# Feeding the feed-forward block product by product, and fewer doubled weight steps, in a fused attention and SwiGLU kernel

## The chip, the cores and the metric

The kernel runs on one core of one Trainium2 chip. The metric is the device time of one execution in microseconds (us). The engines are named as in the profile: PE is TensorE (matmul), PEld its weight loads, DVE is VectorE, ACT is ScalarE, POOL is GpSimd, SP the queue of SyncE.

## The reference

Attention with a threshold, followed by a feed-forward block of SwiGLU type, all results in float32:

```python
# q, k, v: (8 batches, 8 heads, 576, 64)
scores = scale * np.matmul(q, k.transpose(0, 1, 3, 2))
thresh = np.max(scores, axis=-1, keepdims=True) - tau
scores = np.where(scores >= thresh, scores, -1000000000.0)
scores = scores - np.max(scores, axis=-1, keepdims=True)
attn = np.exp(scores)
attn = attn / (np.sum(attn, axis=-1, keepdims=True) + 1e-09)
out = np.matmul(attn, v)
x = out.transpose(0, 2, 1, 3).reshape(4608, 512)
g = x @ w_gate                       # 512 x 1536
silu = g * (1.0 / (1.0 + np.exp(-g)))
val = x @ w_val                      # 512 x 1536
result = silu * val @ w_out          # 1536 x 512
```

The three weight matrices come as 64-bit floating-point numbers.

## The kernel before, in words

**Two programs in one.** The attention half runs in tiles of scores; the block (the feed-forward half) is cut into small pieces and put between them, so that PE has work while the other engines do the softmax of a tile. One block unit is 256 rows of x. There are 18 units. Each has six groups of two feature strips of 128: for each group a gate product sum (`pg`), then a value product sum (`pv`), each of eight products (two strips, four pieces of the 512 inputs). One such product is a matmul of 128x128 by 256 columns, and the profile counts two instructions for it. After the gate sums ACT writes tanh(g/2) and g/2 (L518, L519); after the value sums DVE computes (tanh + 1) x value (L525); and `gates` multiplies with g/2 on GpSimd (L537). The outputs of the first two units are 24 products of 512 columns each (`output`, L574); the others take a scheme of seven block products (`seven`, L607) for which sums of weights and of hidden values are formed first.

**The tiles.** This text counts tiles of scores from T0 in the order of the program. The loop at the end goes over segments (a pair of heads) and the tiles in them:

- T0 to T7: batch 0, the first two tiles of each of four pairs, in which weights arrive and no block work exists yet
- T8 to T19: batch 0 again, three tiles for each of the four pairs (T10, T13, T16 and T19 are the short ones, 64 query rows of each head, `t == NT`)
- T20 to T159: seven batches of four segments, each of four full tiles and then the short one (T24, T29, T34 and so on). In each segment there is one tile in which the attention-times-values products of the segment before (`xa`, L469, 72 instructions) also run.

In batch 0 the tiles are normalised and transposed on PE (`flip`: `tp` and `end`) and multiplied with v soon after (`attend_tile`). In the later batches DVE transposes them in blocks of 32 (L394).

**A tile** has these steps: scores on PE (L311 in batch 0, L303 later) into two PSUM tiles, of which there are only two; maximum on DVE (L338 or L326, then an exchange between partitions, L276); exponential on ACT (L345); multiplication by the mask on DVE with a sum (L349), which is the last reader of the scores; the reciprocal sum, and the scaling on ACT and POOL (L357, L355).

**How the block is fed.** `block` is a generator. It yields the cost of what it has put out, and `fill(n)` draws from it until a credit of n is used up. A product of 256 columns costs 1. The main loop calls `fill(part)` twice in each tile, with `part` from `pace`, which spreads the block work at hand over the tiles that are still to come. What is drawn beyond the credit is taken from the next tile's. Block matmuls use PSUM tiles of one pool of four (`ps_f`), shared with the transposes and the value products.

**How the weights come.** There are 24 pieces of 128x768 values. `fetch_weights` starts the transfer of a piece. `split_weights` takes its two 32-bit halves on ACT (L193, L194), into the destination and into one of two buffers (`los`). `join_weights` puts the bits together with three DVE operations (L200, L204, L207) and an addition on POOL (L209), which is the last reader of the buffer. Sixteen pieces are for gate and value weights, eight for output weights. In an ordinary tile one piece is split and one joined. In the short tiles of T8 to T19 two are joined and a second one is split at the end of the tile.

All four engine queues are written in the order in which the program calls the operations; no scheduler moves them.

Of the kernel before, what the change touches and what calls it, by code (L numbers as in the profile page):

```python
# [19 lines left out]
def kernel(  # L20
# [30 lines left out]
    nc = tc.nc  # L51
    P = 128
    B, H, S, D = q.shape
    NP = H // 2
    DM, DFF = w_gate.shape
    NCC = DM // P
    NF = DFF // P
# [7 lines left out]
    NT = SM // P  # L65
    SH = S // 2
    TC = 256
# [98 lines left out]
    NW = len(wpieces)  # L166
# [332 lines left out]
    def rows_of_products(j, cs, f, mat, name):  # L499
        n = cs.stop - cs.start  # L500
        ps = ps_f.tile([P, 512], F32, name=name, tag="psf")[:, 0:GR * n].rearrange("p (f n) -> p f n", n=n)
        x = xts[j].rearrange("p c t a r -> p c (t a r)")
        for i in range(GR):
            for c in range(NCC):
                nc.tensor.matmul(ps[:, i], wgv[:, mat, c, (f + i) * P:(f + i + 1) * P], x[:, c, cs],  # L505
                                 start=(c == 0), stop=(c == NCC - 1))
            if i < GR - 1:
                yield HCOST
        return ps

    def gate(j, cs, f, hts, gts):
        if f // 2 not in hts:
            hts[f // 2] = hp.tile([P, 2, TC], F32, name="ht") if j != ("full", 0) else hfirst[:, f:f + 2, :]
        gts[f] = gp.tile([P, GR, TC], F32, name="gt"), tp_.tile([P, GR, TC], F32, name="tn")
        need(NCC * ((f + GR - 1) * P // FW + 1))
        ps = yield from rows_of_products(j, cs, f, 0, "pg")

        nc.scalar.activation(gts[f][1], ps, AF.Tanh, scale=0.5)  # L518
        nc.scalar.activation(gts[f][0], ps, AF.Copy, scale=0.5)  # L519
        yield HCOST  # L520

    def value(j, cs, f, hts, gts):
        ps = yield from rows_of_products(j, cs, f, 1, "pv")
        gt, tn = gts.pop(f)
        nc.vector.scalar_tensor_tensor(out=hts[f // 2], in0=tn, scalar=1.0, in1=ps, op0=ALU.add, op1=ALU.mult)  # L525
        ungated.append((hts, f // 2, gt))
        if f == NF - GR and cs.stop == TC:
            del xts[j]
        if f >= NF - 2 * GR and not ready:

            gates()
        yield HCOST

    def gates():
        eng = nc.vector if attended else nc.gpsimd
        for hts, x, gt in ungated:
            eng.tensor_tensor(out=hts[x], in0=hts[x], in1=gt, op=ALU.mult)  # L537
        for hts, x, gt in ungated:
            if hts["seven"] and x >= NF2 // 2:

                ht = hts[x]
                x -= NF2 // 2
                fs = slice(2 * x, 2 * x + 2)
                h11, h21 = hts[x][:, :, 0:P], hts[x][:, :, P:2 * P]
                eng.tensor_tensor(out=hs3[:, fs], in0=h11, in1=h21, op=ALU.subtract)
                eng.tensor_tensor(out=h21, in0=h21, in1=ht[:, :, P:2 * P], op=ALU.add)
                eng.tensor_tensor(out=hs2[:, fs], in0=h21, in1=h11, op=ALU.subtract)
        ungated.clear()

    OF = 3  # L550

    def send(unit, i, ob):

# [11 lines left out]
    def output(unit):  # L565
        hts = hidden[unit]
        for i in range(TC // P):
            po = ps_f.tile([P, 512], F32, name="po", tag="psf")[:, 0:DM].rearrange("p (e n) -> p e n", e=2)
            for f in range(NF):
                if f % OF == 0:  # L570
                    if any(u[0] is hts for u in ungated):
                        gates()
                    need(NW)
                nc.tensor.matmul(po, hts[f // 2][:, f % 2, i * P:(i + 1) * P], wo[:, :, f, :],  # L574
                                 start=(f == 0), stop=(f == NF - 1))
                if f == NF - 1:
                    ob = op.tile([P, 2, DM], F32, name="ob")
                    nc.scalar.copy(ob[:, i].rearrange("p (e n) -> p e n", e=2), po)
                    send(unit, i, ob[:, i])
                if f % OF == OF - 1:  # L580
                    yield OCOST

    w11, w12, w21, w22 = (wo[:, e, f * NF2:(f + 1) * NF2, :] for f in range(2) for e in range(2))

# [8 lines left out]
    def seven(unit):  # L593

        hts = hidden[unit]
        if any(u[0] is hts for u in ungated):
            gates()
        ob = op.tile([P, 2, DM], F32, name="ob")
        o11, o12, o21, o22 = (ob[:, i, e * DM2:(e + 1) * DM2] for i in range(2) for e in range(2))

        def block_of(y, i):
            return lambda f: hts[(y * NF2 + f) // 2][:, f % 2, i * P:(i + 1) * P]

        def product(h, w):
            ps = ps_f.tile([P, 512], F32, name="po", tag="psf")[:, 0:DM2]
            for f in range(NF2):
                nc.tensor.matmul(ps, h(f), w[:, f, :], start=(f == 0), stop=(f == NF2 - 1))  # L607
            return ps

        def add(o, x, y):  # L610
            nc.vector.tensor_tensor(out=o, in0=x, in1=y, op=ALU.add)

        nc.scalar.copy(o12, product(block_of(0, 0), w11))
        yield SCOST
        nc.scalar.copy(o21, product(block_of(1, 1), ws4))
        yield SCOST
        add(o11, o12, product(block_of(1, 0), w21))
        for x in range(NF2 // 2):
            h12 = hts[NF2 // 2 + x][:, :, 0:P]
            nc.gpsimd.tensor_tensor(out=h12, in0=h12, in1=hs2[:, 2 * x:2 * x + 2], op=ALU.subtract)  # L620
        yield SCOST
        add(o12, o12, product(lambda f: hs2[:, f, :], ws2))
        yield SCOST
        add(o22, o12, product(lambda f: hs3[:, f, :], ws3))
        nc.gpsimd.tensor_tensor(out=o21, in0=o21, in1=o22, op=ALU.add)
        yield SCOST
        ps = product(block_of(0, 1), w12)
        add(o22, o22, ps)
        add(o12, o12, ps)
        send(unit, 1, ob[:, 1])  # L630
        yield SCOST
        add(o12, o12, product(block_of(1, 0), w22))
        send(unit, 0, ob[:, 0])
        yield SCOST

    EARLY = 4
    HCOST, OCOST, SCOST = NCC, OF * DM / TC, NF2 * DM2 / TC
    hidden = {}  # L640
    ready = deque()

# [3 lines left out]
    FIRST, SECOND = unit_of("full", 0), unit_of("full", 1)  # L646

    def cost(unit):
        outs = 0 if unit == FIRST else 4 * NF // OF * OCOST if unit == SECOND else 7 * SCOST
        return 2 * NF * HCOST + outs  # L650

    def outputs(unit):
# [153 lines left out]
    for n, seg in enumerate(segs):  # L806
        if NP <= n < 2 * NP:
            seg["v"] = segs[seg["i"]]["v"]
        for x, t in enumerate(seg["tiles"]):
            go = scores(seg, t)  # L810
            next(go)
            next(last, None)
            attends = prev is not None and x == 1
            products = iter(())
            attend_tile()
            next(go)
            next(last, None)
            flip()
            if n == NP and x == 0:
                attend_tile()  # L820
                give(n - 1)
            if n == 2 * NP and x == 1:
                give(n - 1)
            if attends and n > 2 * NP:
                if prev["i"] % NP == 0:
                    need(NW)
                    start_batch(prev["i"] // NP)
                products = attend(prev)
            part = pace(n, x) / 2
            more = len(split)  # L830
            if n or x:
                split_weights()
                fetch_weights(2)
            if x == 0 and n >= NP:
                fetch_qk(seg["i"] + 1)
            next(go)
            if more and not (t == NT and NP <= n < 2 * NP):
                join_weights()
            fill(part)
            next(go)  # L840
            fill(part)
            gates()
            last = go
            if n == NP and later:
                to, fr = later.pop(0)
                nc.vector.transpose(out=to, in_=fr)
            if t == NT and NP <= n < 2 * NP:

                join_weights(2)
                split_weights()  # L850
                fetch_weights(2)
            if attends and n > 2 * NP:
                next(products)
                next(products)
                give(n - 1)
            if attends and seg["halved"]:
                load_v(seg)
            if x == 0 and 0 < n < NP:
                load_v(seg)
            if x == len(seg["tiles"]) - 2 and n + 1 < len(segs):  # L860
                prepare(segs[n + 1])
                if n < NP:
                    fetch_qk(segs[n + 1]["i"] + 1)
        prev = seg
# [42 lines left out]
```

## Time and profile before

| | before |
|---|---|
| time, median of 3 runs | 1526.37 us (1525.08 to 1527.90) |
| span of the profiled execution | 1524.4 us |
| PE busy | 1483.4 us (97%) |
| PEld busy | 1126.8 us (74%) |
| DVE busy | 995.6 us (65%) |
| ACT busy | 726.8 us (48%) |
| POOL busy | 645.5 us (42%) |
| gate and value products on PE (L505) | 399.8 + 399.9 us |
| seven-product outputs on PE (L607) | 176.2 us |
| scores on PE (L303) | 157.5 us |
| attention times values on PE (L469) | 128.8 us |

PE is nearly full over the whole span, so a shorter time can only come from where it is not, or from where its clock is low. The page's second part cuts the span into 40 slices of about 38 us, with the busy tenths of each engine and the clock that PE was granted. A table of windows gives the same for stretches that one chooses; a line of waits gives the engine and line that waited, what it waited for, the sum in us, how often, and the longest; the chain of waits goes back from the last instruction, or from the end of a window, to what released each step.

### The profile page before, as it was taken

The numbers are of one execution on the slowest core, as the hardware profiler recorded it, in microseconds if no ns is written. First come the engines' busy times: TensorE is split into PE (matmuls) and PEld (weight loads), VectorE is DVE, ScalarE is ACT, GpSimd is POOL, SyncE is SP. The second block draws the span as 40 slices with busy tenths as digits, with TensorE's granted clock in tenths as the row PEclk, the third lists the DMA queues.
The fourth block names the chain that finished last, engine by engine and source line by source line (L and its number), as shares of the span: only waits on it lengthen the run. The fifth ranks groups of instructions, "written<-read, shape, count | busy, mean of one in ns | idle before, by whom it ended". The sixth has DMA issues, their size and how long they took to land.

```text
span 1524.4 us, 31468 instructions
## 1 busy us (share of the span) xinstructions
PE 1483.4 (97%) x11784; PEld 1126.8 (74%) x11784; DVE 995.6 (65%) x3038; ACT 726.8 (48%) x2157; POOL 645.5 (42%) x638
## 2 busy tenths in 40 slices
PE   7998899899999999999999999999999999999999
PEld 5776564477777777787777777777777777888887
DVE  6877888867767777756666676767676776512212
ACT  5877555545445455444545545544544454311100
POOL 3355543348453545435444545444545353500000
PEclk9999999999999999999999999999999999999999
DMA  9543221111212011111101121211101120000000
GB/s 195 143 146 104 63 46 46 46 40 32 46 18 53 11 31 46 46 32 32 28 22 45 33 46 32 46 32 46 31 21 28 46 48 15 1 15 1 14 14 15
DMA packets 176872, 66.93 MB, mean 44 GB/s; under 512 B 159696, under 2 KB 159696, under 8 KB 176720
## 3 DMA queue, kind: packets, MB, share of 16 engines
q1 hardware_dynamic: 169552, 56.45, 16.3%
q0 software_dynamic: 2432, 7.87, 1.4%
q8 instruction: 94, 1.54, 0.4%
q10 hardware_dynamic: 4736, 0.59, 0.3%
q14 instruction: 58, 0.48, 0.1%
HBM read 55.44 MB, written 9.44 MB: 43 GB/s over the span
## 4 chain that ended last, share of the span: by engine, by line
PE 89%; DVE 6%; ACT 2%; issue 1%; DMA 1%; POOL 1%; SPq 0%; DVEq 0%; ACTq 0%; POOLq 0%
PE pv L505 23%; PE pg L505 23%; PE po L607 19%; PE sc L303 9%; PE xa L469 8%; PE po L574 2%; PE sc L311 1%; DVE pall L349 1%; PE tp L417 1%; DVE mx L326 1%; DVE pall L394 1%; PE xa L443 1%; ACT pall L345 1%; DVE mx L276 1%; DVE wo L207 0%
## 5 line engine op out<-in xcount | busy, mean ns | idle before, releaser
L355 POOL TENSOR_SCALAR pall<-pall,ri 128x288 f32<-128x288 f32 (+1 forms) x260 | 265.9, 1032 | 319.7 <-DVE ri L365 289.7
L505 PE MATMUL pg<-xall,wgv 128*128 128x256 f32 x1728 | 399.8, 382 | 0.7 <-ACT pall L423 0.6
L505 PE MATMUL pv<-xall,wgv 128*128 128x256 f32 x1728 | 399.9, 382 | 0.0
L505 PEld LDWEIGHTS pg<-xall,wgv 128*128 128x128 f32 x1728 | 323.5, 190 | 67.0 <-issue 20.6
L505 PEld LDWEIGHTS pv<-xall,wgv 128*128 128x128 f32 x1728 | 324.5, 190 | 63.3 <-issue 20.5
L326 DVE TENSOR_REDUCE mx<-sc 128x2 f32<-128x576 f32 x252 | 180.2, 750 | 205.7 <-PE sc L303 204.1
L349 DVE SCALAR_TENSOR_TENSOR pall<-sc,th,pall 128x288 f32<-128x288 f32 (+1 forms) x540 | 258.1, 528 | 33.2 <-ACT pall L345 33.2
L345 ACT ACTIVATE pall<-sc,nm 128x288 f32<-128x288 f32 (+1 forms) x540 | 236.8, 511 | 0.6
L341 ACT ACTIVATE th<-nm,cut 128x4 f32<-128x4 f32 (+1 forms) x140 | 41.6, 297 | 373.2 <-DVE nm L330 373.2
L537 POOL TENSOR_TENSOR ht<-ht,gt 128x512 f32<-128x512 f32 x84 | 106.8, 1271 | 212.1 <-DVE ht L525 137.4
L394 DVE STREAM_TRANSPOSE pall<-pall 128x576 f32<-128x576 f32 x252 | 181.4, 754 | 0.1
L607 PE MATMUL po<-wo,ht 128*128 128x256 f32 x768 | 176.2, 382 | 0.0
L303 PE MATMUL sc<-kT,qT 64*32 64x288 f32 x4032 | 157.5, 410 | 17.4 <-DVE pall L349 16.1
L525 DVE SCALAR_TENSOR_TENSOR ht<-tn,pv 128x512 f32<-128x512 f32 x102 | 69.9, 685 | 155.1 <-PE pv L505 148.6
L607 PEld LDWEIGHTS po<-wo,ht 128*128 128x128 f32 x768 | 144.3, 190 | 27.7 <-issue 5.6
L518 ACT ACTIVATE tn<-pg 128x512 f32<-128x512 f32 x108 | 64.8, 600 | 152.0 <-PE pg L505 145.5
L357 ACT ACTIVATE pall<-pall,ri 128x288 f32<-128x288 f32 (+1 forms) x264 | 132.8, 553 | 0.0
L279 ACT COPY sums<-sums 32x4 f32<-32x4 f32 (+1 forms) x560 | 108.5, 194 | 48.5 <-DVE pall L349 37.8
L469 PE MATMUL xa<-pall,vall 64*64 64x288 f32 x2016 | 128.8, 405 | 0.2 <-ACT pall L345 0.2
L303 PEld LDWEIGHTS sc<-kT,qT 64*32 64x32 f32 x4032 | 59.0, 105 | 94.2 <-issue 68.8
L469 PEld LDWEIGHTS xa<-pall,vall 64*64 64x64 f32 x2016 | 75.9, 133 | 49.0 <-issue 4.1
L620 POOL TENSOR_TENSOR ht<-ht,xall 128x256 f32<-128x256 f32 x48 | 34.6, 729 | 168.9 <-PE po L607 166.9
(101 smaller groups left out, 1338.5 us busy)
## 6 DMA issues: line engine op xcount, KB each, us to landing
vall<-in_v_dram SPq DMA_DIRECT2D x112, 144.0 KB, 3.4
qraw<-in_q_dram SPq DMA_DIRECT2D x116, 72.0 KB, 2.4
kraw<-in_k_dram SPq DMA_DIRECT2D x116, 72.0 KB, 2.8
out_dram<-ob POOLq DMA_DIRECT2D x28, 256.0 KB, 2.4
wo<-in_moe_w_gate_dram SPq DMA_DIRECT2D x16, 384.0 KB, 3.6
wo<-in_moe_w_val_dram SPq DMA_DIRECT2D x16, 384.0 KB, 4.3
xall<-in_moe_w_out_dram SPq DMA_DIRECT2D x5, 768.0 KB, 4.8
wo<-in_moe_w_out_dram SPq DMA_DIRECT2D x3, 768.0 KB, 4.6
```

Source lines behind the costliest of these rows:

```text
L279: nc.scalar.copy(out, in_[:, :, 0])
L303: nc.tensor.matmul(ps[g * G:(g + 1) * G, h, 0:SH], qT[hs, col + a * G:col + (a + 1) * G], kT[hs, c * SH:(c + 1) * SH], start=True, stop=True)
L326: nc.vector.tensor_reduce(out=mx[:, 2 * x:2 * x + 2, 0], in_=tile_[:, :, 0:SH], axis=AX.X, op=ALU.max, negate=True)
L345: nc.scalar.activation(ps[x], scs[x], AF.Exp, bias=nm[:, x:x + 1])
L349: nc.vector.scalar_tensor_tensor(out=ps[x], in0=scs[x], scalar=th[:, x:x + 1], in1=ps[x], op0=ALU.is_ge, op1=ALU.mult, accum_out=sm[:, x, ...
L355: nc.gpsimd.tensor_scalar(out=ps[x], in0=ps[x], scalar1=ri[:, x:x + 1], scalar2=None, op0=ALU.mult)
L357: nc.scalar.activation(ps[x], ps[x], AF.Copy, scale=ri[:, x:x + 1])
L394: nc.vector.transpose(out=p, in_=p)
L469: nc.tensor.matmul(xa[a][h * D:(h + 1) * D, at:at + n * G].rearrange("d (i q) -> d i q", q=G), vr[rs, h, j, :], p[rs, lo:lo + n, j, :], st ...
L505: nc.tensor.matmul(ps[:, i], wgv[:, mat, c, (f + i) * P:(f + i + 1) * P], x[:, c, cs], start=(c == 0), stop=(c == NCC - 1))
L537: eng.tensor_tensor(out=hts[x], in0=hts[x], in1=gt, op=ALU.mult)
L607: nc.tensor.matmul(ps, h(f), w[:, f, :], start=(f == 0), stop=(f == NF2 - 1))
```

## The change

The generator now yields after every product in place of after four products (gate and value sums), three output products of 512 columns (`output`, cost 6) or six products of the seven-product scheme (cost 6). The sums of the costs are the same. It is for spreading the block evenly over the tiles, which before got multiples of four or six.

The doubled weight step is kept only in the short tiles of the first two segments of batch 0 (T10 and T13); T16 and T19 become ordinary tiles, with one split and one join. Where the step is doubled, it now stands ahead of `gates()`, so that the additions of the join come before the gate multiplications in POOL's queue.

```diff
@@ rows_of_products
             for c in range(NCC):
                 nc.tensor.matmul(ps[:, i], wgv[:, mat, c, (f + i) * P:(f + i + 1) * P], x[:, c, cs],
                                  start=(c == 0), stop=(c == NCC - 1))
-            if i < GR - 1:
-                yield HCOST
+                if (i, c) != (GR - 1, NCC - 1):
+                    yield 1
         return ps
@@ gate, value
-        yield HCOST
+        yield 1
@@ output
             for f in range(NF):
-                if f % OF == 0:
-                    if any(u[0] is hts for u in ungated):
-                        gates()
-                    need(NW)
+                if any(u[0] is hts for u in ungated):
+                    gates()
+                need(NW)
...
-                if f % OF == OF - 1:
-                    yield OCOST
+                yield OCOST
@@ seven
             for f in range(NF2):
                 nc.tensor.matmul(ps, h(f), w[:, f, :], start=(f == 0), stop=(f == NF2 - 1))
+                if f < NF2 - 1:
+                    yield SCOST
             return ps
...
-        nc.scalar.copy(o12, product(block_of(0, 0), w11))
+        ps = yield from product(block_of(0, 0), w11)
+        nc.scalar.copy(o12, ps)
         yield SCOST
...
-    HCOST, OCOST, SCOST = NCC, OF * DM / TC, NF2 * DM2 / TC
+    HCOST, OCOST, SCOST = NCC, DM / TC, DM2 / TC
@@ main loop
             next(go)
-            if more and not (t == NT and NP <= n < 2 * NP):
+            double = t == NT and NP <= n < NP + 2
+            if more and not double:
                 join_weights()
             fill(part)
             next(go)
             fill(part)
+            if double:
+
+                join_weights(2)
+                split_weights()
+                fetch_weights(2)
             gates()
             last = go
             if n == NP and later:
                 to, fr = later.pop(0)
                 nc.vector.transpose(out=to, in_=fr)
-            if t == NT and NP <= n < 2 * NP:
-
-                join_weights(2)
-                split_weights()
-                fetch_weights(2)
```

More of the change, by code (lines that the diff above doesn't have):

```diff
@@ L531, in value @@
             gates()
-        yield HCOST
+        yield 1
     def gates():
@@ L548, in gates @@
         ungated.clear()
-    OF = 3
     def send(unit, i, ob):
@@ L611, in add @@
             nc.vector.tensor_tensor(out=o, in0=x, in1=y, op=ALU.add)
-        nc.scalar.copy(o12, product(block_of(0, 0), w11))
+        ps = yield from product(block_of(0, 0), w11)
+        nc.scalar.copy(o12, ps)
         yield SCOST
-        nc.scalar.copy(o21, product(block_of(1, 1), ws4))
+        ps = yield from product(block_of(1, 1), ws4)
+        nc.scalar.copy(o21, ps)
         yield SCOST
-        add(o11, o12, product(block_of(1, 0), w21))
+        ps = yield from product(block_of(1, 0), w21)
+        add(o11, o12, ps)
         for x in range(NF2 // 2):
@@ L621, in seven @@
         yield SCOST
-        add(o12, o12, product(lambda f: hs2[:, f, :], ws2))
+        ps = yield from product(lambda f: hs2[:, f, :], ws2)
+        add(o12, o12, ps)
         yield SCOST
-        add(o22, o12, product(lambda f: hs3[:, f, :], ws3))
+        ps = yield from product(lambda f: hs3[:, f, :], ws3)
+        add(o22, o12, ps)
         nc.gpsimd.tensor_tensor(out=o21, in0=o21, in1=o22, op=ALU.add)
         yield SCOST
-        ps = product(block_of(0, 1), w12)
+        ps = yield from product(block_of(0, 1), w12)
         add(o22, o22, ps)
@@ L631, in seven @@
         yield SCOST
-        add(o12, o12, product(block_of(1, 0), w22))
+        ps = yield from product(block_of(1, 0), w22)
+        add(o12, o12, ps)
         send(unit, 0, ob[:, 0])
@@ L648, in cost @@
     def cost(unit):
-        outs = 0 if unit == FIRST else 4 * NF // OF * OCOST if unit == SECOND else 7 * SCOST
+        outs = 0 if unit == FIRST else 4 * NF * OCOST if unit == SECOND else 7 * NF2 * SCOST
         return 2 * NF * HCOST + outs
```

## The prediction

> **What bounds the kernel now.** I read the slices of the page first, to see where TensorE (PE) is not full:
>
> ```profile
> PE   7998899899999999999999999999999999999999
> DVE  6877888867767777756666676767676776512212
> PEclk9999999999999999999999999999999999999999
> ```
>
> From the ninth slice on (38 us each) PE is at 90% or more; VectorE (DVE) is fuller before it than after. The table of windows puts numbers to that, with stage borders that I chose: the first eight tiles, the rest of batch 0 (T8 to T19), the first six tiles of batch 1 (T20 to T25), the rest of batch 1, batches 2 to 7, the tail.
>
> ```profile
> 0.00:62.00 62.00, 50.23 (x367) 37.41 (x368) 46.26 (x104) 43.63 (x95) 20.66 (x18) 1.00 0.81 185
> 62.00:153.00 91.00, 82.89 (x598) 64.01 (x596) 69.32 (x135) 68.69 (x133) 48.24 (x27) 0.96 0.37 120
> 153.00:196.00 43.00, 35.83 (x337) 25.03 (x342) 38.63 (x116) 25.62 (x72) 25.13 (x19) 0.96 0.34 74
> 196.00:310.00 114.00, 105.81 (x954) 57.46 (x958) 88.39 (x299) 62.97 (x207) 41.60 (x40) 0.99 0.18 42
> 310.00:1330.00 1020.00, 1017.78 (x8615) 777.03 (x8608) 708.61 (x2302) 502.99 (x1602) 499.29 (x520) 1.00 0.15 34
> 1330.00:1525.00 195.00, 190.80 (x934) 165.89 (x933) 44.43 (x85) 22.95 (x50) 10.61 (x15) 1.00 0.04 12
> ```
>
> Columns after the length: busy us of PE, PEld, DVE, ACT, POOL, then PE clock. PE idles 8.1, 7.2 and 8.2 us in the second to fourth row and 2.2 us in the 1020 us after; the first row has no block products and the last idles at the very end, so the change reaches neither. PE waits from 62 to 310 us:
>
> ```profile
> PE sc L303 <- DVE pall L349: 14.1, 9, 3.4
> PE sc L311 <- DVE pall L349: 7.2, 3, 4.6
> PE sc L303 <- PE sc L303: 0.8, 5, 0.2
> PE pg L505 <- ACT pall L423: 0.6, 1, 0.6
> ```
>
> Nearly all is one thing: the scores of the next tile wait until the multiplication by the mask (L349) has read the scores of this one. That PSUM pair is fully used by one tile, so PE gets past it only if its block products last as long as the chain of maximum, exponential and mask. The chain of waits for the longest of them:
>
> ```profile
> 125.63 0.69 DVE extra L525
> 126.32 2.02 DVE wo L200 x2
> ...
> 131.05 1.63 POOL wo L209
> 132.68 0.02 issue
> 132.70 0.99 ACT extra L194
> ...
> 134.03 0.64 ACT pall L345
> 134.67 0.02 issue
> 134.70 0.84 DVE pall L349 x2
> 135.53 0.14 issue
> 135.67 3.28 PE sc L311 x9
> ```
>
> A doubled join (DVE 126.3 to 131.0) comes before GpSimd's addition; the second split on ScalarE (ACT, L194) waits for that addition to free its buffer, and the exponential of the next tile stands behind it. Meanwhile PE had only four products and waited 4.62 us.
>
> **What the Trainium skill says.** "PSUM — Partial Sum Buffer", section Engine vs sequencer instructions: ACT, DVE and GpSimd queues are strict FIFO, and matmuls start and complete in program order. The chain above agrees: exponentials for a tile that was ready stand 1.6 us behind L194. "TensorE: Matmul & The Clock Gate", part 1, What's actually happening: after an idle window of about 3.4 us the PE clock goes to half, and comes back after a busy one. The trace agrees: clock 0.50 over 135.6 to 142.4 us (after the 4.62 us wait), 0.51 over 162.8 to 166.2 (after 3.37) and 0.50 over 299.4 to 302.8: 13.6 us at half, 6.8 us lost. "Perfetto Trace Analysis", Optimization Strategy: repeating bubbles on an engine that should be saturated can mean that PSUM for the next tile ran out. Here that is the score pair.
>
> **The change part by part.**
>
> *Single products, counted.* In the trace a product of 128x128 by 256 columns takes 3.45/8 = 0.43 us (tail, start to start); an output product of 512 columns counts as two. Per tile, before: T9 to T20 get 8 8 4, 8 8 4, 8 8 4, 8 8 4; T21 to T26 get 8 12 8 12 8 8. After, by the changed program's issue order: 7 7 7, 7 6 7, 7 7 7, 7 6 7 and 10 9 10 9 10 9; in T27 to T41 the spread of 6 to 12 becomes 8 to 10, and later 8 to 18 becomes 13 to 15 almost everywhere. Sums agree within 4 products at stage borders. No product is added; the few switches between scores and block keep their number, so I cost the finer steps themselves at nothing.
>
> *T8 to T19.* To win: 8.1 us idle and 3.4 of clock, 11.5. The waits ahead of T12, T15, T18 (1.55, 1.00, 4.62) follow the tiles of four products. The doubled joins of T16 and T19 go; a single join (0.5+0.5+0.9 plus gaps, 2.1 us of DVE) then sits ahead of L525, no second split stands in ACT's queue, and a tile there is 3.5 us of scores, transposes and values plus 7 x 0.43 = 6.5 us of PE, against 4.6 us from the start of the scores to the end of both L349 (68.57 to 73.2). So T18's wait and its slow clock vanish. T12 and T15 keep doubled joins: three products more in the tile ahead take 1.3 us, but two fewer come in the tiles before that, so I leave 0.65 and 0.55. In T10 the multiplication L525 now lies ahead of the join on DVE (+0.6), which is in that 0.65. The join ahead of GpSimd's gate multiplications (1.28 us each) keeps these off L209, for which ACT waits; they are read only by outputs about 100 us later: nothing.
>
> *A new wait here:* a half-done sum holds one of four PSUM buffers through the flip, which wants four. PE then stands in order behind ACT's copy, as at T12 (0.62). I count 0.6 and 0.3 as they stand in T12 and T15, and as new 0.6, 0.5 and 0.3 in T10, T16 and T18; bounds zero and twice the new ones. What remains is 0.65 + 0.55 + 0.9 + 1.4 = 3.5 us. T20 starts with two products fewer done (0.9). Gain 11.5 - 3.5 - 0.9 = 7.1.
>
> *T20 to T25.* Here DVE is busy 38.6 of 43 us, so it sets the pace. A full tile costs it 5.73 us from scores to scores (212.15 to 217.88: maxima 1.3, sums and exchange 1.2, transposes 1.35, two of four masks 0.9, start 0.8). A join adds 2.1, L525 0.6. The two joins taken from T16 and T19 now come in T22 and T24. Following DVE tile by tile: T20 6.5 (PE sets it, the 3.37 us wait gone), T21 7.55, T22 8.4, T23 7.9, T24 and T25 together 13.6, in sum 43.9 against 43.0 (152.99 to 195.94). Three more products are done (1.3). Gain 0.4: what T20 wins is paid back. PE may wait 3.3 us in T22 and lose its clock, but it has slack there.
>
> *T26 to T41.* A tile of ten products is 1.13 + 4.3 = 5.4 us for PE, so DVE's 5.73 sets it; where both k and q are transposed and a short tile follows, the pair takes about 12.0 (with L525) or 11.0 us. Tiles with the 72 value products (4.53) are PE's own. Credited with the products done: T26 +0.2, T27 to T30 24.7 to 23.4 with two fewer, +0.4; T31 +0.5; T32 to T36 33.5 to 31.7 with two fewer, +0.9; T37 to T41 37.0 to 32.4, +4.6, of which 1.7 is the clock loss at 299.4. Gain 6.7, rounded up from these.
>
> *Later.* 2.2 us of idle in 1020; with 13 products at least in every tile I expect about 1.6 of it. The yields inside the seven products of an output only move their place between tiles; PE stays full.
>
> Sum: 7.1 + 0.4 + 6.7 + 1.6 = 15.8 us, less a little for waits that I can't see: 1526.4 - 15.4 = 1511.0.
>
> **The rivals.** *A, DVE keeps the time.* Even products bring nothing where the DVE chain sets the pace, half-done sums stand in the way, and only the two removed doubled joins count: 4.62 idle + 3.4 clock, minus 0.9: 1519. For it: DVE 88.4 of 114 us busy in T26 to T41. Against it: DVE waits there for scores (3.35 us at 206.46, 0.8 at most others), after overfull tiles. *B, all idle is won:* 8.1 + 7.2 + 8.2 + 2.2 and 6.8 of clock, 32.5: 1494. Against it: 38.6 of 43 us DVE, with two joins more. *C, slower:* PSUM buffers held by half sums cost the copy wait of 0.6 in each of the 12 flips and of the 28 tiles with value products (24 us), which eats the 15.4: 1535. For it: one such wait exists. Against it: half sums were held in every second tile before, and the wait shows once. *D, no change,* 1526: gain and buffer waits cancel.
>
> **How the numbers follow.** Main 0.66, A 0.19, B 0.05, C 0.06, D 0.04. Faster: main, A and B, 0.90. The low end: if the 3.5 us left in T8 to T19 vanish, and T26 to T41 give all of their 8.2 idle and 1.7 of clock in place of 6.7, it is 6.7 us less, 1504.3, rounded to 1505. The high end takes in A, 1520. Outside lie B, C, D and the edges of the main case, about 2 in 10.
>
> **What would show it.** In the changed profile: PE busy unchanged near 1483 less the slow-clock time (about 5 us); no half clock at 135; no wait of PE over 1 us between T16 and T20; PE waiting 2 to 3 us ahead of T23 and T24 on L349, with a join just before; waits under 2 us ahead of T27 to T41, each after a short tile or a tile of eight products. A row of PE pg or pv waiting for ACT L423 or DVE L525 of more than 4 us in total would make C's mechanism real; idle in the batches 2 to 7 above 4 us would make the forecast wrong, and so would scores of T26 that start later than 192 us (195.94 before).

## The result and the profile after

| | before | changed |
|---|---|---|
| time, median of 6 runs each | 1527.13 us (1525.08 to 1528.51) | 1514.70 us (1513.19 to 1516.52) |
| span of the profiled execution | 1524.4 us | 1512.9 us |

The ratio is 0.992, with a 95% interval of 0.9907 to 0.9933: faster by 12.4 us, under one per cent but clear of the noise. The forecast was 1511.0 us with a range of 1505 to 1520.

The page of the changed kernel, the row of busy times and three rows of the 40 slices:

```profile
PE 1480.5 (98%) x11784; PEld 1121.3 (74%) x11784; DVE 994.8 (66%) x3038; ACT 727.1 (48%) x2157; POOL 643.3 (43%) x638
...
PE   7999899999999999999999999999999999999999
...
DVE  6878988777777777747767666776666767512212
...
PEclk9999999999999999999999999999999999999999
```

After the first slice only the fifth (151 to 189 us) has PE under 90%; it is also the one in which DVE stands at 90% or more. The table of windows with the same kind of borders (columns as before: length, busy us of PE, PEld, DVE, ACT, POOL, clock, DMA share, GB/s):

```profile
62.00:152.00 90.00, 85.11 (x663) 63.85 (x662) 70.42 (x141) 68.97 (x136) 48.65 (x28) 1.00 0.37 120
152.00:192.00 40.00, 33.48 (x296) 23.04 (x300) 36.99 (x113) 27.21 (x74) 22.54 (x18) 0.96 0.40 87
192.00:310.00 118.00, 113.22 (x1035) 60.54 (x1020) 94.03 (x316) 68.64 (x227) 44.88 (x43) 1.00 0.18 40
310.00:1318.00 1008.00, 1007.50 (x8509) 770.33 (x8510) 703.06 (x2282) 497.03 (x1581) 496.92 (x518) 1.00 0.16 34
```

PE now idles 4.9, 6.5, 4.8 and 0.5 us in these rows; before it was 8.1, 7.2, 8.2 and 2.2. The clock is down in one of these rows instead of three; one more stretch at half clock lies ahead of them (last section). The waits of PE from 62 to 310 us:

```profile
PE sc L303 <- DVE pall L349: 10.1, 12, 2.6
PE pv L505 <- ACT pall L423: 2.7, 3, 1.4
PE sc L303 <- PE sc L303: 0.9, 6, 0.2
PE sc L311 <- DVE pall L349: 0.9, 1, 0.9
```

Three things are to be seen. The waits of batch 0 for the mask (L311) fall from 7.2 us to 0.9. A new row of 2.7 us has come: value sums wait for ACT to empty a PSUM buffer. And the waits of the later batches (L303) are more in number, 12 for 9, but shorter.

The same in lengths from the start of one tile's scores to another's, in the profiled executions. This table also holds the experiments, and the next section refers to it:

| kernel | time, us | ratio to before (95%) | T8 to T20 | T20 to T26 | T26 to T42 | T42 to end |
|---|---|---|---|---|---|---|
| before | 1527.13 | 1 | 95.82 | 42.95 | 114.64 | 1213.84 |
| changed | 1514.70 | 0.992 (0.9907 to 0.9933) | 89.02 | 43.38 | 110.50 | 1211.56 |
| e1_single_only | 1517.30 | 0.9933 (0.9921 to 0.9945) | 92.03 | 43.90 | 110.50 | 1211.55 |
| e2_joins_only | 1521.66 | 0.996 (0.9948 to 0.9973) | 90.06 | 43.12 | 112.99 | 1213.80 |
| e3_coarse_batch0 | 1514.61 | 0.9917 (0.9903 to 0.993) | 88.86 | 42.52 | 110.95 | 1211.55 |
| e4_coarse_late | 1515.05 | 0.9918 (0.9906 to 0.993) | 89.25 | 43.42 | 110.50 | 1212.25 |
| e5_gates_first | 1515.32 | 0.9921 (0.9908 to 0.9935) | 90.25 | 43.39 | 110.50 | 1211.54 |
| e6_no_double | 1513.75 | 0.991 (0.9897 to 0.9923) | 84.32 | 45.53 | 112.23 | 1211.53 |
| e7_joins_t26 | 1516.40 | 0.9927 (0.9914 to 0.9939) | 89.56 | 40.15 | 116.81 | 1211.52 |
| e8_coarse0_joins_t26 | 1516.72 | 0.9925 (0.9913 to 0.9938) | 90.01 | 39.29 | 115.68 | 1211.54 |
| e9_hold_two_t26 | 1514.89 | 0.9917 (0.9901 to 0.9933) | 89.17 | 40.38 | 114.29 | 1211.52 |
| e10_nodouble_hold_one | 1511.73 | 0.9895 (0.9878 to 0.9913) | 84.32 | 45.57 | 110.30 | 1211.51 |
| e11_nodouble_hold_two | 1515.12 | 0.9916 (0.99 to 0.9932) | 84.33 | 45.29 | 112.92 | 1211.54 |
| e12_no_turn | 1516.24 | 0.9926 (0.9903 to 0.9949) | 89.17 | 43.39 | 110.56 | 1211.55 |

Each ratio is taken against runs of the kernel before beside it on the same chip (medians of these: 1527.66 for e1 to e4, 1527.82 for e5 to e8, 1526.57 for e9 to e12). Between before and changed the stages differ by -6.80, +0.43, -4.14 and -2.28 us; T8 itself starts 1.28 us later, 0.93 of it for a reason in the last section. The sum, -11.5, is the difference of the spans.

### The profile page after: what moved, and what is told of

Read it like the earlier page. It is cut to its first block, busy times and chain, and to the rows that moved or that the text cites. A ratio compares the mean times of both kernels' runs of the same rounds, so it can differ in the third digit from the quotient of the medians.

```text
span 1512.9 us, 31439 instructions
## 1 busy us (share of the span) xinstructions
PE 1480.5 (98%) x11784; PEld 1121.3 (74%) x11784; DVE 994.8 (66%) x3038; ACT 727.1 (48%) x2157; POOL 643.3 (43%) x638
## 5 line engine op out<-in xcount | busy, mean ns | idle before, releaser
L355 POOL TENSOR_SCALAR pall<-pall,ri 128x288 f32<-128x288 f32 (+1 forms) x260 | 265.9, 1032 | 344.8 <-DVE ri L365 317.9
L505 PE MATMUL pv<-xall,wgv 128*128 128x256 f32 x1728 | 404.9, 383 | 3.0 <-ACT pall L423 2.7
L326 DVE TENSOR_REDUCE mx<-sc 128x2 f32<-128x576 f32 x252 | 180.6, 751 | 237.4 <-PE sc L303 236.6
L349 DVE SCALAR_TENSOR_TENSOR pall<-sc,th,pall 128x288 f32<-128x288 f32 (+1 forms) x540 | 258.1, 528 | 31.6 <-ACT pall L345 31.6
L537 POOL TENSOR_TENSOR ht<-ht,gt 128x512 f32<-128x512 f32 x84 | 107.1, 1275 | 193.1 <-DVE ht L525 109.6
L394 DVE STREAM_TRANSPOSE pall<-pall 128x576 f32<-128x576 f32 x252 | 181.4, 754 | 2.8 <-POOL pall L355 2.8
L303 PE MATMUL sc<-kT,qT 64*32 64x288 f32 x4032 | 158.4, 411 | 11.3 <-DVE pall L349 10.1
L525 DVE SCALAR_TENSOR_TENSOR ht<-tn,pv 128x512 f32<-128x512 f32 x102 | 69.9, 685 | 132.3 <-PE pv L505 119.0
L303 PEld LDWEIGHTS sc<-kT,qT 64*32 64x32 f32 x4032 | 58.8, 106 | 89.0 <-issue 61.0
```

The lines of the kernel that those rows point to most:

```text
L303: nc.tensor.matmul(ps[g * G:(g + 1) * G, h, 0:SH], qT[hs, col + a * G:col + (a + 1) * G], kT[hs, c * SH:(c + 1) * SH], start=True, stop=True)
L326: nc.vector.tensor_reduce(out=mx[:, 2 * x:2 * x + 2, 0], in_=tile_[:, :, 0:SH], axis=AX.X, op=ALU.max, negate=True)
L349: nc.vector.scalar_tensor_tensor(out=ps[x], in0=scs[x], scalar=th[:, x:x + 1], in1=ps[x], op0=ALU.is_ge, op1=ALU.mult, accum_out=sm[:, x, ...
L355: nc.gpsimd.tensor_scalar(out=ps[x], in0=ps[x], scalar1=ri[:, x:x + 1], scalar2=None, op0=ALU.mult)
L394: nc.vector.transpose(out=p, in_=p)
```

## The experiments

**Which half does what: e1 and e2.** The first keeps the single products and puts the joins back, the second the reverse.

```diff
e1, against the changed kernel
-            double = t == NT and NP <= n < NP + 2
-            if more and not double:
+            if more and not (t == NT and NP <= n < 2 * NP):
...
-            if double:
-
-                join_weights(2)
-                split_weights()
-                fetch_weights(2)
             gates()
...
+            if t == NT and NP <= n < 2 * NP:
+
+                join_weights(2)
+                split_weights()
+                fetch_weights(2)
e2, against the changed kernel (value, output and seven likewise)
-                if (i, c) != (GR - 1, NCC - 1):
-                    yield 1
+            if i < GR - 1:
+                yield HCOST
```

> Single products as in the changed kernel; doubled joins in T10, T13, T16 and T19, behind the gate multiplications, as before. My theory: from T26 on it is the changed kernel (6 us of gain there), but T18 keeps a wait of about 3.5 us (4.6 less three products) with the slow clock behind it, and T21 one of about 2; T22 to T25 have two joins fewer than the changed kernel. 1517 to 1520 us. Rival 'the joins are the change': 1523 or more. Rival 'the single products are all': within 1 us of the changed kernel (1514.7).

> Steps of four and six products as before; doubled joins only in T10 and T13 and ahead of the gate multiplications, as in the changed kernel. My theory: the 4.62 us ahead of T18 and its slow clock go (8 us), T21's wait halves, T23 to T25 pay for the two later joins (3 to 4 us), T26 to T41 and later stay as before: 1519 to 1522 us. Rival 'the joins are the change': 1515. Rival 'the single products are all': 1526.

The stages part cleanly. With single products alone, T26 to T42 and all after are the changed kernel's to 0.01 us, and T8 to T20 wins 3.8 us. With the joins alone, T42 to the end is that of before, and T8 to T20 wins 5.8. A stretch at half clock (114.6 to 118.0 us) is in that one: T15 takes 9.08 us where e3, with the same steps there, takes 7.83. Without these 1.25 us it would be 88.8, the changed kernel's 89.0. e3 below, which is e2's program up to T19, has no such stretch and takes 88.86. So in batch 0 the joins do all of it, and the single products are one of two cures for the same wait: the 4.62 us ahead of T18's scores are gone in e1, in e2 and with both. Inside T18 PE waits 1.53 us in e1, 0.62 in e2 and 0.57 with both. That is why 10.4 us (e1) and 6.0 (e2) are together 12.4 and not 16.4. (e1's time came inside its range, but the wait of 3.5 us ahead of T18 that was expected with it did not come.) PE's waits in e1 from 62 to 200 us show what single products bring with them while the joins stay doubled:

```profile
PE pv L505 <- ACT pall L423: 2.9, 3, 1.4
PE pv L505 <- ACT xall L449: 2.7, 2, 1.4
```

The second row is not among the changed kernel's to that size (0.3): ACT's copy of a tile's values stands behind a split, which waits for an addition on POOL.

The changed kernel's PE around T18, from its timeline (start, length, line, operation, instructions):

```profile
130.85 1.13 PE L505 MATMUL pv<-xall,wgv 128*128 128x256 f32 x4
131.82 2.32 PE L505 MATMUL pg<-xall,wgv 128*128 128x256 f32 x10
134.07 1.36 PE L311 MATMUL sc<-pall 64*128 64x288 f32 x10
```

There are seven products where there were four (x14 for x8), and the scores follow at once; no bracket with a wait stands in the row of L311. The 0.57 us that the tile still waits come later, between two of its sums, for ACT's copy (L423).

**Are the single products worth anything in batch 0? e3. And late? e4.**

```diff
+    step = {"fine": True}
...
-                if (i, c) != (GR - 1, NCC - 1):
+                if fine and (i, c) != (GR - 1, NCC - 1):
                     yield 1
+            if not fine and i < GR - 1:
+                yield HCOST
...
+        step["fine"] = n >= 2 * NP
e4: the same with the last line
+        step["fine"] = n <= 3 * NP
```

> The changed kernel, but with steps of four products for block groups that begin in T8 to T19. My theory: the even products win about 1 us each at T12 and T15 and the waits for PSUM copies that half-done sums cost there take 3 us, so T20 starts within 1 us of the changed kernel (147.5 us) and the time is 1514 to 1516 us. Rival 'even products are what wins in batch 0': T20 starts 2 us later or more, 1517. Rival 'half-done sums cost': T20 starts 2 us earlier, 1512.

> The changed kernel, but with steps of four and six products from T45 on. My theory: PE is full there with or without, 1 to 2 us are lost in two or three waits of about 1 us as before (at 414 and 480 us): 1515.5 to 1517 us. Rival 'finer steps cost PE something by themselves' (partial sums in more PSUM buffers, more switches): faster than the changed kernel by 1 us or more.

In e3 the waits for the mask at T12 and T15 are back, and those for PSUM copies at T9, T11 and T16 are gone. PE's waits from 62 us to T20, e3:

```profile
PE sc L311 <- DVE pall L349: 2.6, 2, 1.6
PE pv L507 <- ACT pall L423: 0.6, 1, 0.6
PE pg L507 <- ACT pall L423: 0.6, 1, 0.6
```

and the changed kernel in the same stretch:

```profile
PE pv L505 <- ACT pall L423: 2.7, 3, 1.4
PE sc L311 <- DVE pall L349: 0.9, 1, 0.9
PE pv L505 <- ACT xall L449: 0.3, 1, 0.3
```

3.8 us against 3.9 in these rows: one wait takes the place of the other, and the time is the same (0.9917 and 0.992). e3 has even done two products more when T20 starts (84 from T8 on, against 82), which the changed kernel makes good by T42, where both have done 288. In e4 0.7 us of the 2.28 that are won after T42 are lost. The other 1.6 stay although the steps are coarse from T45 on: PE's waits after T42 are 0.3 us in e4 and 2.2 before. Why the coarse steps do not bring those waits back is open.

**The order of join and gates: e5.**

```diff
             fill(part)
+            gates()
             if double:
...
-            gates()
```

> The changed kernel with one thing undone: where the step is doubled (T10, T13), the gate multiplications stand ahead of the join again. My theory after the run of the single products alone, where T11 waited 1.38 us in place of 0.31: the end of the first value sum now lies in T10, its multiplication (1.28 us on GpSimd) then holds up the addition for which the second split on ScalarE waits; T12 starts 1.1 to 1.3 us later, nothing else moves: 1515.5 to 1516.5 us. Rival (the prediction's 'nothing'): 1514.5.

By time nothing can be told (0.9921 and 0.992, the intervals all but the same). In the trace one wait grows: PE ahead of T12, e5 and then the changed kernel, from the timelines:

```profile
88.11 1.99 PE L505 MATMUL pv<-xall,wgv 128*128 128x256 f32 x8 [1.38 <-ACT xall L449]
```

```profile
88.35 1.99 PE L505 MATMUL pv<-xall,wgv 128*128 128x256 f32 x8 [0.31 <-ACT xall L449]
```

1.07 us, and T8 to T20 is 1.23 longer. The expectation put this on POOL's queue, where the multiplication would hold up the addition. The timelines show another way. In e5 POOL is idle for 2.30 us between the two, because the addition waits for the join on DVE:

```profile
80.43 2.11 DVE L200 TENSOR_SCALAR wgv<-wgv 128x768 f32<-128x768 f32 x2
80.66 1.46 POOL L537 TENSOR_TENSOR extra<-extra,gt 128x512 f32<-128x512 f32 x1 [3.32 <-ACT wgv L193]
84.42 4.23 POOL L209 TENSOR_TENSOR wgv<-wgv,extra 128x768 uint32<-128x768 uint32 x2 [2.30 <-DVE wgv L207]
```

The same join in the changed kernel, with no multiplication beside it:

```profile
81.75 1.02 DVE L200 TENSOR_SCALAR wgv<-wgv 128x768 f32<-128x768 f32 x2
84.72 4.16 POOL L209 TENSOR_TENSOR wgv<-wgv,extra 128x768 uint32<-128x768 uint32 x2 [6.07 <-DVE wgv L207]
```

The multiplication (L537) lengthens the first step of the join from 1.02 to 2.11 us; the addition, ACT's split and the copy behind it then come later by as much. The last section has more on this. In the kernel before, the joins ahead of T18 and T20 were stretched in the same way (2.10 us ahead of T18).

**The doubled joins that are left, and where the last joins should be: e6, e7, e9, e10, with e8 and e11 as their pairs.** e6 drops the two doubled joins too. e7 and e8 keep the joins of T22 and T24 for T25 and T26 (e8 with e3's steps in batch 0). e9 puts two joins at the end of T26, behind the value products and both fills. e10 joins e6 with one of them there, e11 with two.

```diff
e6
-            double = t == NT and NP <= n < NP + 2
+            double = False
e7
+            held = n == 2 * NP and x >= 2
-            if more and not double:
+            if more and not double and not held:
e9
-        if fetched:
+        if fetched and len(split) < 2:
...
-                    need(NW)
...
+            held = (n == 2 * NP and x >= 2) or (n == 2 * NP + 1 and x < 2)
...
+                if prev["i"] % NP == 0:
+                    need(NW)
e10: e6, and e9 with
+            held = n == 2 * NP + 1 and x < 2
```

> The changed kernel with no doubled join at all. My theory: the 0.5 and 0.86 us ahead of T12 and T15 and ScalarE's blocking go (1.5 us), two more joins come in T25 and T26, the first on a full VectorE (2 us), the second in a tile with value products where VectorE has slack: within 1 us of the changed kernel. Rival 'doubled joins are only harm': 1512. Rival 'pieces come too late and the block waits for weights': 1518 or more.

> The changed kernel with the joins of T22 and T24 held back to T25 and T26, whose value products give VectorE 4 us of slack. My theory (VectorE sets the pace in T22 to T25, and those joins cost 2.1 us each there): T23 to T26 take 2.5 to 3.5 us less, T26 to T27 at most 0.5 more: 1511.5 to 1512.5 us. Rival 'PE or PSUM sets the pace there, joins are hidden': 1514.5.

> Both together: steps of four products for groups begun in T8 to T19, and the two joins held back to T25 and T26. The first alone was within 0.1 us of the changed kernel, so the theory says as with the second alone, 1511.5 to 1512.5 us.

> The changed kernel with the joins of T22 and T24 held back past T25 to the end of T26, behind its masks and its block products and ahead of the copies of its value products. In the run that did one of them in T25 and one ahead of T26's masks, T23 to T26 took 2.6 us less, but T26 waited 3.3 us ahead of its value products and 3.33 ahead of its second half of scores, with a slow clock behind. My theory: those waits came from joins standing ahead of the transposes that the value products read; here VectorE is free from the masks of T26 to the scores of T27, and 4.2 us fit: T26 as early as there, T26 to T27 about 10.2 us: 1511.5 to 1512.5 us. Rival 'the joins cost as much wherever they stand': 1514.5 or more.

> No doubled join at all, and the last two joins (T25, T26) at the end of T26 as in the run beside it. Without doubled joins T20 came 4.7 us earlier and 4 us were lost from T20 to T27, 2 of them in T25 and T26. Theory: T20 to T27 takes 2 us less than there: 1511 to 1512 us. Rival 'VectorE's work is only moved, its sum decides': 1513.75 as there.

> As the run beside it, with the join of T24 held too, and a piece split only while fewer than two wait for their join, so that the last joins fall together at the end of T26. Theory: T24 to T26 lose another 2 us of VectorE, T26 to T27 stays within 1 us: 1509.5 to 1511 us, the fastest of all. Rival 'three or more joins at one place block it': 1512 or more.

e6 wins 4.7 us up to T20, and gives 3.9 back by T42: the two pieces not joined in batch 0 are joined later. The last falls in T26, by `need(NW)` ahead of the transposes that the value products read; ACT's scaling, the value products and PE stand behind it (1.59 us).

e7 shows the same at larger size. T20 to T26 is 3.2 us shorter, so the joins there do cost what they seem to; T26 takes it all back, and a half clock on top (PE's timeline):

```profile
195.59 7.61 PE L469 MATMUL xa<-pall,vall 64*64 64x288 f32 x72 [3.33 <-ACT pall L357]
```

The 72 value products took 4.60 us in e10. e8 ends the same way, also with its coarse steps.

e9 has no such wait in T26, but T28's scores wait 3.40 us, with a half clock from 204.6 to 211.4 us around them. DVE's timeline behind T26's masks:

```profile
194.51 0.55 DVE L200 TENSOR_SCALAR wo<-wo 128x768 f32<-128x768 f32 x1
195.10 1.51 DVE L204 TENSOR_SCALAR wo<-wo 128x768 uint32<-128x768 uint32 x1
196.64 0.96 DVE L207 SCALAR_TENSOR_TENSOR wo<-xall,wo 128x768 uint32<-128x768 uint32 x1
197.52 0.55 DVE L200 TENSOR_SCALAR wo<-wo 128x768 f32<-128x768 f32 x1
198.11 2.05 DVE L204 TENSOR_SCALAR wo<-wo 128x768 uint32<-128x768 uint32 x1
200.20 0.96 DVE L207 SCALAR_TENSOR_TENSOR wo<-xall,wo 128x768 uint32<-128x768 uint32 x1
201.07 1.41 DVE L326 TENSOR_REDUCE mx<-sc 128x2 f32<-128x576 f32 x2
```

The scores of T27 began at 197.33, and their maximum (L326) could begin only at 201.07, behind both joins. In e10 one join stands there:

```profile
195.53 0.56 DVE L200 TENSOR_SCALAR wo<-wo 128x768 f32<-128x768 f32 x1
196.12 1.50 DVE L204 TENSOR_SCALAR wo<-wo 128x768 uint32<-128x768 uint32 x1
197.66 0.96 DVE L207 SCALAR_TENSOR_TENSOR wo<-xall,wo 128x768 uint32<-128x768 uint32 x1
199.16 1.42 DVE L326 TENSOR_REDUCE mx<-sc 128x2 f32<-128x576 f32 x2 [0.54 <-PE sc L303]
```

Here DVE is through before the scores are: it waits 0.54 us for them. So while PE does T26's value products (4.6 us) there is room for one join and not for two; e11, with two and no doubled joins, again has waits of 3.54 us at T28. The rivals that e9 and e11 were given came true (1514.5 or more, 1512 or more). e10 is the fastest version of the study: 1511.73 us (1511.21 to 1511.94), 0.9895 (0.9878 to 0.9913), about 3 us below the changed kernel. The two ratios' intervals overlap a little; each of e10's five runs lies below each of the changed kernel's six, though on another chip, and below all of e9's and e11's on its own.

**What sets the pace from T27 on: e12.** The transposes of the attention weights (L394) are left out for the batch's later segments, so what is attended there is not the reference's.

```diff
-                unturned.append([seg["p"][:, x, :] for x in at])
+            if not NP + 1 <= seg["i"] < 2 * NP:
+                unturned.append([seg["p"][:, x, :] for x in at])
```

> The changed kernel without the block transposes on VectorE (two of 0.68 us in each tile) for the tiles of three segments, T25 to T39: the attention of those pairs is then computed from untransposed weights, so the result differs from the reference. Theory (VectorE's chain from scores to masks sets the pace in T27 to T41, not PE): the exponential's wait of 0.85 us takes the place of 1.35 us, 0.4 to 0.5 us for each of 15 tiles as far as PE has room: T27 to T42 3 to 6 us shorter. Rival 'PE is the bound there, at 0.44 us for a product between other work': no change.

Nothing became shorter: T27 to T42 is 100.43 us against 100.37. From 200.1 to 300.5 us of each execution DVE is busy 66.08 us in place of 82.39, PE 95.57 in place of 95.62. DVE in the short tile T29, first the changed kernel:

```profile
216.98 0.16 DVE L330 TENSOR_REDUCE nm<-mx 128x2 f32<-128x4 f32 x1
217.06 1.43 DVE L394 STREAM_TRANSPOSE pall<-pall 128x576 f32<-128x576 f32 x2
218.41 0.48 DVE L349 SCALAR_TENSOR_TENSOR pall<-sc,th,pall 128x288 f32<-128x288 f32 x1
```

and e12:

```profile
215.63 0.16 DVE L330 TENSOR_REDUCE nm<-mx 128x2 f32<-128x4 f32 x1
216.99 0.52 DVE L349 SCALAR_TENSOR_TENSOR pall<-sc,th,pall 128x288 f32<-128x288 f32 x1 [1.20 <-ACT pall L345]
```

From the maximum (L330) to the mask (L349) it is 1.43 us with the transposes and 1.36 without. In T27 to T40 this stretch takes 1.31 to 1.50 us with the transposes and 1.30 to 1.50 without. They lie in the time in which DVE would wait for ACT's exponential anyway, so the work that DVE has in a tile does not set the pace.

What does set it is not one thing, and the rival has a part in it. At the end of the full tiles of ten products (T28, T32, T37, T38) PE waits at most 0.16 us for the next tile's scores: there PE itself is the bound, as the rival said, with scores that it takes in halves as the masks release them. T27 and T33, with nine and eight products, end in waits of 0.49 and 0.71 us for the mask, and in e12 of 0.49 and 0.76. There the loop of scores, maximum, exponential and mask through two engines is the bound, and the transposes are not on it.

Of the twelve, e1, e2, e3, e6 and e10 came inside the times that were expected; e4 and e5 took 0.5 and 0.2 us less; e7, e8, e9, e11 and e12 missed.

## Why the prediction was right, and where it was off

The direction and the range held; the gain was 12.4 us and not 15.4. The mechanism held in part: evener products and fewer doubled joins took away the waits for the mask. In batch 0, however, the single products win nothing beside the joins, and from T26 on PE's own time was set too low. The stages of the forecast were too high by 1.2 us (T8 to T19) and 3.0 (T26 to T41), and too low by 0.5 (T20 to T25) and 0.7 (the rest); that these errors partly cancel is luck.

**T8 to T19.** Forecast: T20 starts 8.0 us earlier (7.1, and 0.9 for two products that it owes); measured 6.80. The signs came: no half clock at 135, no wait over 1 us from T16 to T20 (0.71 the longest). Of the other signs, PE was busy 1480.5 us (forecast about 1478), T26's scores started at 190.85 (limit 192), and PE's idle time in batches 2 to 7 was 0.5 (limit 4). Waits left in T9 to T19 sum to 4.3 us, forecast 3.5. The new PSUM waits were put at T10, T16 and T18; they came at T9 (1.40), T11 (0.31), T16 (0.71) and T18 (0.57). Ahead of T12 and T15 PE waits 0 and 0.86 us, forecast 0.65 and 0.55. The division of the gain was wrong: the step that gave T12 and T15 something for "three products more in the tile ahead" stands in the trace, but what it wins the new waits take (e3), and the whole gain is that of the joins (e2).

**The order of the join was costed at "nothing".** e5 shows 1.07 us in the wait ahead of T12, in the trace alone. The prediction looked at who reads the gated values, and saw that the order "keeps these off L209, for which ACT waits". It did not see that the multiplication also stretches the join on DVE, and that is what costs the 1.07 us.

**T20 to T25.** Followed tile by tile: forecast 6.5, 7.55, 8.4, 7.9 and 13.6 us for T20 to T25, measured 6.59, 7.39, 8.28, 7.61 and 13.51. The longest wait came at T23 as forecast (2.60 us, with half clock from 170.2 to 173.4 us behind it; no time is lost by that, since T23 takes 7.61 us in e5 too, where the clock stays up). At T24 it was 0.16 in place of 2 to 3, with 1.34 at T25. DVE's timeline ahead of T23 shows the forecast order, mask, join, L525, maximum of the scores that had long been there:

```profile
162.10 0.56 DVE L200 TENSOR_SCALAR wo<-wo 128x768 f32<-128x768 f32 x1
...
164.16 0.68 DVE L525 SCALAR_TENSOR_TENSOR extra<-tn,pv 128x512 f32<-128x512 f32 x1
164.76 1.42 DVE L326 TENSOR_REDUCE mx<-sc 128x2 f32<-128x576 f32 x2
```

**T26 to T41: the term that was mis-sized.** Forecast 6.7 us with the products done counted in. The stage became 4.14 us shorter with one product fewer done (0.43), so 3.7 is what compares with it. The step that failed is "1.13 + 4.3 = 5.4 us for PE, so DVE's 5.73 sets it". T28 in PE's timeline:

```profile
206.76 0.72 PE L303 MATMUL sc<-kT,qT 64*32 64x288 f32 x16 [0.49 <-DVE pall L349]
207.63 0.72 PE L303 MATMUL sc<-kT,qT 64*32 64x288 f32 x16 [0.16 <-PE sc L303]
208.28 2.43 PE L505 MATMUL pv<-xall,wgv 128*128 128x256 f32 x10
210.55 2.32 PE L505 MATMUL pg<-xall,wgv 128*128 128x256 f32 x10
212.80 0.71 PE L303 MATMUL sc<-kT,qT 64*32 64x288 f32 x16
```

From 208.28 to 212.80 ten products take 4.5 us and not 4.3: the 0.43 us of one product was read where products follow one another, and between scores ten of them take 4.49 to 4.56. The scores take 1.13 us only where PE comes late and finds both score tiles free, as in the tile of before from which 5.73 was read. Where PE comes first, it takes one as soon as it is released and waits for the other, and then the scores take 1.53 (206.76 to 208.28). So PE alone needs 5.65 to 6.04 us, and T29's scores follow T28 without a wait.

The six full tiles of this kind (T27, T28, T32, T33, T37, T38) took 5.78 to 6.04 us, 5.90 in the mean, which is 1.0 us in sum. The pairs of a short tile and the next took 0.3 more than forecast in sum. T36 and T41, with value products, were forecast at 9.2 and 9.9 us (31.7 and 32.4, less two full tiles and a pair of 11.0 each) and took 9.59 and 10.54, which is 0.9; the last has waits of 0.85 ahead of it. T26 and T31 took 0.43 and 0.80 us more for one and two products more, so they gained next to nothing (forecast 0.7). That is the missing 3.0.

Moreover 1.7 us, in the forecast and in the measured gain alike, are the half clock at 299.4 of the one execution before: in e2 the same waits of 1.90 us stand ahead of T41 and the clock stays up, so this share need not be the change's. The parts that the prediction gave for the 5.73 add up to 5.55, and "transposes 1.35" does not belong among them, since DVE waits as long for the exponential without them (e12).

**Later.** Forecast 1.6 us of idle, and 0.5 is left of 2.2, so 1.7 came. The other 0.6 of the 2.28 is open; both kernels have done 288 products when T42 starts, so it is not work moved ahead.

**The rivals.** A (only the joins count, 1519) is e2's case in batch 0, but e1 wins 6.4 us after T26, and 4.7 of them (2.5 to T42 against e2, 2.2 later) no join gives. C's buffer waits are real and small: pv and pg for L423 in all 2.9 us, below the 4 that were named. B would have needed the joins of T20 to T25 to be free; e7 and e9 show that moving them off that stage costs as much elsewhere, e10 that one of them has a free place.

## What to carry to other kernels

Two edits that each remove the same wait do not add up: build each alone before dividing the gain, or their sum will be promised. A piece of work has to be priced where it will stand: a product costs 0.43 us in a row of products and 0.45 between scores, and scores cost 1.13 us in two free tiles and 1.53 in tiles that are released one after the other. Whether an operation is on the loop can be tested by leaving it out. And work that must be done somewhere, as these weight joins, is free only in a gap of the engine that is longer than the work in its worst company: here one join fits beside 72 value products, and two do not.

## What the runs showed of the hardware

**DVE and GpSimd stop one another.** L204 (one instruction of a join) takes 0.55 or 0.56 us in most places, but 1.51 and 2.05 in e9's lines above. GpSimd's timeline there:

```profile
194.74 1.45 POOL L537 TENSOR_TENSOR ht<-ht,gt 128x512 f32<-128x512 f32 x1 [2.45 <-ACT sums L279]
197.68 2.06 POOL L209 TENSOR_TENSOR wo<-wo,extra 128x768 uint32<-128x768 uint32 x1 [1.49 <-DVE wo L207]
```

Each L204 begins within one of these and ends 0.42 us after it (196.61 and 196.19; 200.16 and 199.74). The Trainium skill, "SBUF — State Buffer", section Who interferes with whom, says that a two-port DVE instruction and GpSimd exclude each other for a whole instruction; these runs agree. So does e5: of its two L200, the second takes 1.64 us in place of 0.55 and ends 0.42 us after L537. It isn't so beside every GpSimd instruction: in the changed kernel L204 takes 0.98 us beside L355 (the scaling) and ends 0.57 us before that one does. The exclusion makes e9's two joins 2.4 us longer (0.95 and 1.49) than two alone, in just the place where they had to be short.

**The half clock falls in one execution and not in another, at the same instructions.** The changed kernel has 3.4 us of it from 47.2 us, in T6, where its program is that of before and PE had waited only 0.81 us; T6 took 7.80 us in place of 6.24, and T6 and T7 together 0.93 longer. None of the twelve experiments has one there (they start T8 anywhere from 56.96 to 58.97 us all the same). In T15, behind the same wait of 1.02 or 1.03 us, e2 and e8 have one and e3 has none. The prediction read its three half clocks as agreeing with an idle window of about 3.4 us. The waits of 4.62 and 3.37 us fit that; the third, at 299.4 us, stood behind waits of 1.74 and 0.16, and those named here were shorter still. So a half clock can come after much shorter waits, and what decides it is not shown.
